# A new hand-written order for the opening of a fused attention and bilinear-FFN kernel

## The chip, the cores and the metric

The kernel runs on one core of one Trainium2 chip, as one launch. The time is device microseconds of that core: the median of three runs, 401.54 us (401.34 to 401.81). Each time is one whole execution; beside it stands one profiled execution whose trace the readings come from.

## What is computed

Attention with a relative-position bias, then a bilinear feed-forward layer, for 8 batches of 8 heads, 576 positions and 64 values a head:

```python
scores = scale * np.matmul(q, k.transpose(0, 1, 3, 2))
scores = scores + bias.transpose(2, 0, 1)[None, :, :, :]   # bias from |i - j|, 32 buckets, per head
attn = softmax(scores)
x = np.matmul(attn, v)            # then heads side by side: x is 4608 x 512
a = x @ w_a                       # 512 x 1536
b = x @ w_b
out = (a * b) @ w_out             # 1536 x 512, float32
```

## The kernel before

Work is cut by batch and pair of heads: 32 pairs, four a batch, numbered p = 0 to 31. For a pair, the 576 positions are four tiles of 128 and a tail of 64. TensorE (PE) makes scores with keys on partitions (`score`, `qk`, `qkh`), ScalarE (ACT) takes their exp into bf16 tiles `at`, VectorE (DVE) multiplies these by the exponential of the bias (tables `W` and `Wt`), and PE multiplies by v with a column of ones beside it (`av`), which yields the sums. DVE divides by the sums into `XG`, and a transpose (on PE, or by DMA on the SP queue) puts the result into `xn`, from which the feed-forward part reads. That part works in chunks of 512 positions: `pa` and `pb` (four matmuls each), ACT copies `pa` into `ha` (L703), DVE multiplies `pb` by `ha` into `g` (L706), and PE multiplies `g` by `wo`.

The program has two stages. The **opening** (batches 0 and 1, pairs 0 to 7, and the first chunk of the feed-forward part) is written out by hand as a list of tokens in the string `opening`. The **steady part** behind it (pairs 8 to 31 and the other chunks) has four lists of its own and is entered with the first `score` matmul. The kernel is built under a manual schedule: each engine issues its instructions in the order in which the tokens stand, and waits at an instruction until its inputs and its buffer are there. So the list's order is the order of each engine's queue.

A token is a kind, numbers and at times an engine, `:A` for ACT and `:D` for DVE:

- `<name`: a load. Nearly all are issued on GpSimd's (POOL's) queue.
- `TQ`, `TK` (L337, L346): PE transposes q or k of a pair into PSUM; `CQ`, `CK` (L327 on ACT, L329 on DVE): the copy out of it. `TZ`, `CZ` (L377) the same for the tails of a batch.
- `S` (`qk_half` L474, `qk` L606), `E` (L480, L458), `M` (L489, L463): scores, their exp, and the multiplication by the bias table. For pairs 0 to 3 these work on halves: `S201` is pair 2, queries' half 0, keys' half 1.
- `KS`, `EK`: scores and exp of the tails' keys for pairs 0 to 3 together.
- `T` (`qk_tail` L507 to L514), `ET` (`ex_tail` L534, L535), `MT` (L551, L543): the same for a pair's tail.
- `AV` (L583 to L593), `N` (L643 to L650): product with v and division. `X` (L672) and `CX`: transposition of the result on PE and the copy into `xn`; for pairs 4 to 6, `N` issues it as DMA transposes on SP's queue (L658, L661).
- `FA`, `HA`, `FB`, `G`: a unit of the feed-forward part: `pa`, `ha`, `pb`, `g`. The suffix is `a` or `b` for a half chunk of 256 positions and `f` for the whole 512.
- `w1`, `w2`: one or two matmuls on zeros, which fill PE's time (`warm`).
- `P..`: writes of zeros into paddings. `V`: copies of v. `LH`, `LV`: loads for batch 2; `TH`: DMA transposes of batch 2's k and q for the steady part.

What ties the tokens to each other is PSUM. One bank, `trb`, has two halves that `tr_half` hands out by turns: to TQ, to TK from pair 4 on, TZ, X, and for pairs 4 to 7 also to a small piece of T (64 tail keys against 64 tail queries, L514). The next but one in this row must wait until the first has been copied out. Scores have two tiles (pool `ps_sc`), `pa` and `pb` two banks (`ps_ff`), `av` one bank. The pieces of T and ET that matter here are:

```python
pt = ps[:, 1, n:n + 2 * ST] if n < SM else tr_half().bitcast(FP32)[:, 0:2 * ST]
nc.tensor.matmul(out=pt, lhsT=z[:, 1, :], rhs=z[:, 0, :], start=True, stop=True)   # L514
...
nc.scalar.activation(out=at[:, m:m + 2 * ST], in_=pt, func=ACTF.Exp, scale=scale)  # L534
```

PE works on different parts of its array in different tokens. Rows and columns in use, as the profile prints them: scores 64*128, transposes of q and k 128*64 (64*64 for q of pairs 0 to 3 but the first), tails' transposes 64*128, all others 128*128.

Of the kernel before, what the change touches and what calls it, by code (L numbers as in the profile page):

```python
# [13 lines left out]
def kernel(  # L14
# [774 lines left out]
    def v_next(s):  # L789
# [7 lines left out]
    ACT = nc.scalar  # L797

    opening = """
        <q123h0 <k1 <tk <vtb <k23 <W1 <W0 <v0 <vta <tq <W2 <W3 <v1 <Wta <q123h1 <R0 <Wtb <R1 <k4 <wa0  # L800
        <wb0 <R2 <uq <q5 <q4 <R3 <k5 <wa1 <q7 <wb1 <k6 <uk <k7 <vb1a <vb1b <vt1a <q6 <wb2 <vt1b <wa2 <wo
        PC0:A PX0:D YQ0:A PC1:A PU0:D PV0:A PX1:D TQ0 YK0:D TK0 CQ00:A CQ01:D CK0:D TQ10 PF1:A CQ10:D
        S000 E000 PV1:D S001 E001 TK1 CK1:D TQ30 TZ1 CZ1:D S011 CQ30:D E011 S101 TQ20 CQ20:D E101 M101
        S100 E100 TK3 CK3:D KS EK M000 TK2 S301 E301 CK2:D w2 S200 E200 M100 M001 w1 S201 E201 V0:D
        PU1:D w2 S300 E300 M200 M201 AV00 TZ0 AV10 S010 CZ0:A N00 T0 N10 E010 X10 X00 CX00:A V1:D AV20
        CX10:A TQ11 TQ21 M301 M300 ET0 AV30 CQ11:A S110 CQ21:A N20 M010 M011 PW:A MT0 S111 TQ31 E110 X20
        CQ31:A E111 T1 ET1 N30 M110 X30 CX20:D CX30:D AV01 T2 TK4 M111 S210 ET2 E210 FA0a HA0a N01 T3
        MT1 X01 AV11 CK4:D CX01:A PF0:D LH ET3 N11 S211 E211 FB0a FA1a HA1a X11 G0a MT2 CX11:D S310 E310
        FB1a G1a S311 M210 FA2a FB2a HA2a E311 TQ5 TQ4 CQ4:A M211 FA3a AV21 CQ5:A S42 G2a S43 FB3a TZ0x
        MT3 M311 HA3a M310 TK5 E42 N21 FA4a HA4a CZ0x:D AV31 LV CK5:D X21 E43 TQ7 CQ7:A G3a N31 S41 E41  # L810
        S52 E52 FB4a FA5a HA5a CX21:D G4a M43 TK6 X31 CX31:D FB5a S40 E40 CK6:D S53 G5a FA0b HA0b TZ1x
        M41 CZ1x:D FB0b G0b S51 E53 FA1b HA1b TK7 FB1b FA2b E51 M52 HA2b CK7:D S50 G1b V2:D FB2b FA3b
        E50 V3:D G2b HA3b T4 M40 FB3b G3b S70 M42 ET4 MT4 FA4b FB4b T5 HA4b M53 E70 G4b TQ6 ET5 M51
        CQ6:A AV40 N40 FA5b S71 E71 S73 MT5 M50 FB5b HA5b AV41 S72 E73 G5b N41 M71 FA6f M73 T6 E72 M72
        ET6 MT6 AV50 FB6f HA6f N50 S62 S61 E62 G6f M62 FA7f HA7f AV51 N51 TH S60 E61 M61 FB7f G7f E60
        M60 S63 E63 FA8f HA8f T7 ET7 M63 M70 FB8f G8f AV60 FA9f FB9f N60 MT7 AV70 HA9f G9f FA10f HA10f
        FB10f N70 AV71 G10f FA11f HA11f FB11f N71 X71 AV61 X70 G11f N61 CX71:D CX70:D
    """

    h0 = (0, 1)  # L820
# [292 lines left out]
```

## Time and profile before

| | |
|---|---|
| median of three runs | 401.54 us |
| the profiled execution | 401.12 us |
| its span | 399.3 us |
| PE busy | 390.6 us, 98% of the span |
| ACT busy | 255.9 us, 64% |
| DVE busy | 240.9 us, 60% |
| first matmul of the feed-forward part | 27.45 us |
| first `score` matmul, where the steady part begins | 70.84 us |

The span runs from the first instruction to the last one of the profile; some 1.8 us of the execution lie around it. Busy time of PE is modelled: a matmul's row lasts longer than its step, since the next one starts before it ends, so the price of a matmul is read from start to start.

### The profile page before, as it was taken

The numbers are of one execution on the slowest core, as the hardware profiler recorded it, in microseconds if no ns is written. First come the engines' busy times: TensorE is split into PE (matmuls) and PEld (weight loads), VectorE is DVE, ScalarE is ACT, GpSimd is POOL, SyncE is SP. The second block draws the span as 40 slices with busy tenths as digits, with TensorE's granted clock in tenths as the row PEclk, the third lists the DMA queues.
The fourth block names the chain that finished last, engine by engine and source line by source line (L and its number), as shares of the span: only waits on it lengthen the run. The fifth ranks groups of instructions, "written<-read, shape, count | busy, mean of one in ns | idle before, by whom it ended". The sixth has DMA issues, their size and how long they took to land.

```text
span 399.3 us, 13162 instructions
## 1 busy us (share of the span) xinstructions
PE 390.6 (98%) x5614; PEld 231.2 (58%) x5626; DVE 240.9 (60%) x565; ACT 255.9 (64%) x386; POOL 133.4 (33%) x199
## 2 busy tenths in 40 slices
PE   6999999999999999999999999999999999999996
PEld 2477655566665666566656665666666654444443
DVE  4799997547754775477756875487547752321420
ACT  4898994568766876587748774777568733323321
POOL 5966531739751885019700880000000000000000
PEclk9999999999999999999999999999999999999999
DMA  8999999899996999729992999161420012002004
GB/s 140 185 204 198 205 158 133 82 188 132 154 152 130 107 168 120 151 57 140 128 123 69 139 122 151 56 99 26 99 80 19 17 29 108 2 26 79 2 0 105
DMA packets 136618, 42.78 MB, mean 107 GB/s; under 512 B 114184, under 2 KB 131816, under 8 KB 136560
## 3 DMA queue, kind: packets, MB, share of 16 engines
q0 software_dynamic: 81120, 19.88, 54.5%
q1 hardware_dynamic: 50096, 12.76, 23.3%
q10 hardware_dynamic: 5344, 9.31, 7.1%
q8 instruction: 44, 0.72, 0.8%
q14 instruction: 14, 0.11, 0.1%
HBM read 39.23 MB, written 9.45 MB: 122 GB/s over the span
## 4 chain that ended last, share of the span: by engine, by line
PE 95%; DMA 1%; ACT 1%; DVE 0%; issue 0%; ACTq 0%; SPq 0%
PE ffn_pair L606 25%; PE ffn L606 24%; PE av L606 8%; PE pb L696 8%; PE pa L696 8%; PE score L606 7%; PE po L733 6%; PE av L589 2%; PE qkh L474 1%; DMA xn<-in_k_dram 1%; PE qk L606 1%; PE qr L444 1%; PE av L583 1%; PE trb L337 1%; PE trk L337 1%; ACT ath L480 0%
## 5 line engine op out<-in xcount | busy, mean ns | idle before, releaser
L458 ACT ACTIVATE at<-score 128x1024 bf16<-128x1024 f32 x96 | 98.4, 1025 | 36.7 <-PE score L606 33.3
L463 DVE TENSOR_TENSOR at<-at,W 128x1024 bf16<-128x1024 bf16 x112 | 74.7, 686 | 26.4 <-ACT at L458 18.1
L606 PE MATMUL ffn_pair<-xn,wb 64*128 64x512 bf16 x288 | 81.8, 376 | 0.0
L606 PE MATMUL ffn_pair<-xn,wa 64*128 64x512 bf16 x288 | 81.8, 376 | 0.0
L606 PE MATMUL ffn<-xn,wa 64*128 64x512 bf16 x288 | 79.9, 377 | 0.0
L606 PE MATMUL ffn<-xn,wb 64*128 64x512 bf16 x288 | 79.6, 375 | 0.0
L606 PE MATMUL av<-vm,at 64*128 64x65 bf16 x1536 | 63.4, 190 | 0.0
L606 PEld LDWEIGHTS <-at 64*128 64x128 bf16 x1536 | 48.8, 94 | 21.8 <-issue 1.2
L606 PEld LDWEIGHTS <-wa 64*128 64x128 bf16 x576 | 47.0, 94 | 17.5
L606 PEld LDWEIGHTS <-wb 64*128 64x128 bf16 x576 | 47.3, 94 | 11.6 <-issue 0.7
L706 DVE TENSOR_TENSOR g<-pb,ha 128x512 bf16<-128x512 f32 (+1 forms) x42 | 25.8, 615 | 44.7 <-PE pb L696 44.2
L606 PEld LDWEIGHTS <-g 64*128 64x128 bf16 x624 | 33.4, 94 | 24.1 <-issue 0.4
L606 PE MATMUL ffn_pair<-wo,g 64*128 64x512 bf16 x336 | 44.0, 376 | 0.0
L703 ACT ACTIVATE ha<-pa 128x512 f32<-128x512 f32 (+1 forms) x42 | 22.6, 538 | 31.9 <-PE pa L696 28.0
L138 POOL DMA_DIRECT2D qn<-in_q_dram x48 | 36.0, 781 | 11.2 <-DMA wo<-in_moe_w_out_dram 7.3
L696 PE MATMUL pb<-xn,wb 128*128 128x512 bf16 (+1 forms) x165 | 37.9, 349 | 0.3
L606 PE MATMUL score<-QB,KB 64*128 64x512 bf16 x192 | 37.9, 376 | 0.0
L696 PE MATMUL pa<-xn,wa 128*128 128x512 bf16 (+1 forms) x163 | 37.5, 348 | 0.2
L147 POOL DMA_DIRECT2D kn<-in_k_dram x48 | 35.8, 759 | 3.4 <-issue 2.2
L606 PE MATMUL av<-vm,att 64*128 64x65 bf16 x384 | 36.6, 190 | 0.0
L706 DVE TENSOR_TENSOR g<-ffn_pair,ha 128x512 bf16<-128x512 f32 x36 | 24.9, 692 | 18.5 <-ACT ha L703 18.0
L606 PE MATMUL ffn<-wo,g 64*128 64x512 bf16 x288 | 35.0, 376 | 0.0
(125 smaller groups left out, 603.1 us busy)
## 6 DMA issues: line engine op xcount, KB each, us to landing
out_dram<-QKT ACTq DMA_DIRECT2D x32, 256.0 KB, 2.0
vn<-in_v_dram POOLq DMA_DIRECT2D x16, 256.0 KB, 5.4
kn<-in_k_dram POOLq DMA_DIRECT2D x48, 64.0 KB, 4.7
qn<-in_q_dram POOLq DMA_DIRECT2D x48, 64.0 KB, 4.2
wa<-in_moe_w_a_dram POOLq DMA_DIRECT2D x3, 512.0 KB, 8.4
wb<-in_moe_w_b_dram POOLq DMA_DIRECT2D x3, 512.0 KB, 8.3
wo<-in_moe_w_out_dram POOLq DMA_DIRECT2D x1, 1536.0 KB, 16.2
xn<-XG SPq DMA_TRANSPOSE x54, 3.9
```

Of the source, the lines that this page charges most:

```text
L138: nc.gpsimd.dma_start(out=by_tile(qn[b % 2])[:, h0 // 4, t, :, :], in_=q[b, h0:h1, 128 * t:128 * t + 128, :].transpose([1, 0, 2]))
L147: nc.gpsimd.dma_start(out=by_tile(kn[b % 2])[:, h0 // 4, t, :, :], in_=k[b, h0:h1, t:SM:NM, :].transpose([1, 0, 2]))
L337: nc.tensor.transpose(ps[64 * hh:64 * hh + 64, 128 * t:128 * t + 128], src[b][:, o:o + 64], ident[:, :])
L444: nc.tensor.matmul(out=rows[hh][:, ST * t:ST * t + ST], lhsT=kT[r, t, :], rhs=z[r, 0, ST * hh:ST * hh + ST], start=True, stop=True)
L458: nc.scalar.activation(out=at[:, :, :], in_=ps[:, :, :], func=ACTF.Exp, scale=scale)
L463: nc.vector.tensor_tensor(out=at[:, :, :], in0=at[:, :, :], in1=w[:, :, S - 1 + t:S - 1 + t - SM:-1], op=MULT)
L589: nc.tensor.matmul(out=pav[:, slot, hh, :], lhsT=weights(p, t, hh, jq), rhs=vm[i][:, 2 * hp + hh, t, :], start=False, stop=True, skip_grou ...
L606: i = nc.tensor.matmul(out=o, lhsT=lhs[r], rhs=rhs[r], start=first, stop=last, skip_group_check=True)
L696: nc.tensor.matmul(out=ps[:, 0:n], lhsT=w[df // 4][:, mc, 128 * (df % 4):128 * (df % 4) + 128], rhs=xn_sb[mc][:, 512 * c + lo:512 * c + lo ...
L703: nc.scalar.activation(out=ha[:, 0:n], in_=ff["pa", df, lo][:, 0:n], func=ACTF.Copy)
L706: nc.vector.tensor_tensor(out=g_sb[df][:, lo:lo + n], in0=ff["pb", df, lo][:, 0:n], in1=ff["ha", df, lo][:, 0:n], op=MULT)
L733: nc.tensor.matmul(out=po[:, :], lhsT=g_sb[df][:, 128 * tt:128 * tt + 128], rhs=wo_sb[:, df, :], start=(df == 0), stop=(df == NDF - 1))
```

## The change

The list `opening` is written anew. Its 357 tokens are the same but for the engine of thirteen copies and pads: CZ0, CX00, CX10, CQ11, CQ31, CX01 and PF1 go from ACT to DVE; CX30, CK5, CX11, CX21, CX71 and CX70 from DVE to ACT. The loads stand first in the same order. All else moves: the order of pairs in the scores, where the feed-forward units stand among them, and that feed-forward units 6, 8 and 10 now come ahead of others with lower numbers. The steady part is unchanged.

```diff
@@ -797,24 +797,26 @@
     ACT = nc.scalar
 
     opening = """
-        <q123h0 <k1 <tk <vtb <k23 <W1 <W0 <v0 <vta <tq <W2 <W3 <v1 <Wta <q123h1 <R0 <Wtb <R1 <k4 <wa0
-        <wb0 <R2 <uq <q5 <q4 <R3 <k5 <wa1 <q7 <wb1 <k6 <uk <k7 <vb1a <vb1b <vt1a <q6 <wb2 <vt1b <wa2 <wo
-        PC0:A PX0:D YQ0:A PC1:A PU0:D PV0:A PX1:D TQ0 YK0:D TK0 CQ00:A CQ01:D CK0:D TQ10 PF1:A CQ10:D
-        S000 E000 PV1:D S001 E001 TK1 CK1:D TQ30 TZ1 CZ1:D S011 CQ30:D E011 S101 TQ20 CQ20:D E101 M101
-        S100 E100 TK3 CK3:D KS EK M000 TK2 S301 E301 CK2:D w2 S200 E200 M100 M001 w1 S201 E201 V0:D
-        PU1:D w2 S300 E300 M200 M201 AV00 TZ0 AV10 S010 CZ0:A N00 T0 N10 E010 X10 X00 CX00:A V1:D AV20
-        CX10:A TQ11 TQ21 M301 M300 ET0 AV30 CQ11:A S110 CQ21:A N20 M010 M011 PW:A MT0 S111 TQ31 E110 X20
-        CQ31:A E111 T1 ET1 N30 M110 X30 CX20:D CX30:D AV01 T2 TK4 M111 S210 ET2 E210 FA0a HA0a N01 T3
-        MT1 X01 AV11 CK4:D CX01:A PF0:D LH ET3 N11 S211 E211 FB0a FA1a HA1a X11 G0a MT2 CX11:D S310 E310
-        FB1a G1a S311 M210 FA2a FB2a HA2a E311 TQ5 TQ4 CQ4:A M211 FA3a AV21 CQ5:A S42 G2a S43 FB3a TZ0x
-        MT3 M311 HA3a M310 TK5 E42 N21 FA4a HA4a CZ0x:D AV31 LV CK5:D X21 E43 TQ7 CQ7:A G3a N31 S41 E41
-        S52 E52 FB4a FA5a HA5a CX21:D G4a M43 TK6 X31 CX31:D FB5a S40 E40 CK6:D S53 G5a FA0b HA0b TZ1x
-        M41 CZ1x:D FB0b G0b S51 E53 FA1b HA1b TK7 FB1b FA2b E51 M52 HA2b CK7:D S50 G1b V2:D FB2b FA3b
-        E50 V3:D G2b HA3b T4 M40 FB3b G3b S70 M42 ET4 MT4 FA4b FB4b T5 HA4b M53 E70 G4b TQ6 ET5 M51
-        CQ6:A AV40 N40 FA5b S71 E71 S73 MT5 M50 FB5b HA5b AV41 S72 E73 G5b N41 M71 FA6f M73 T6 E72 M72
-        ET6 MT6 AV50 FB6f HA6f N50 S62 S61 E62 G6f M62 FA7f HA7f AV51 N51 TH S60 E61 M61 FB7f G7f E60
-        M60 S63 E63 FA8f HA8f T7 ET7 M63 M70 FB8f G8f AV60 FA9f FB9f N60 MT7 AV70 HA9f G9f FA10f HA10f
-        FB10f N70 AV71 G10f FA11f HA11f FB11f N71 X71 AV61 X70 G11f N61 CX71:D CX70:D
+        <q123h0 <k1 <tk <vtb <k23 <W1 <W0 <v0 <vta <tq <W2 <W3 <v1 <Wta <q123h1 <R0 <Wtb <R1 <k4
+        <wa0 <wb0 <R2 <uq <q5 <q4 <R3 <k5 <wa1 <q7 <wb1 <k6 <uk <k7 <vb1a <vb1b <vt1a <q6 <wb2
+        <vt1b <wa2 <wo
+        PC0:A PX0:D YQ0:A PC1:A PU0:D PV0:A PX1:D TQ0 YK0:D TK0 CQ00:A CQ01:D TK1 CK0:D TQ10 S000
+        TQ20 CQ10:D CK1:D S001 E000 TK2 CQ20:D S100 E001 TZ1 E100 S101 PV1:D CK2:D CZ1:D E101 M000
+        TK3 M100 S200 E200 TQ30 M101 S010 E010 V0:D CQ30:D w2 S201 PU1:D KS E201 CK3:D w1 EK S300
+        TZ0 E300 M200 M001 w2 S301 M201 AV10 CZ0:D T0 V1:D AV00 E301 TQ21 S011 ET0 M300 N10 M301
+        N00 CQ21:A TQ11 S210 X10 E011 CQ11:D E210 AV20 X00 S211 M010 AV30 M011 N20 CX10:D PW:A E211
+        CX00:D MT0 T1 ET1 X20 CX20:D N30 TQ31 LH S111 AV01 CQ31:D MT1 E111 X30 M111 CX30:A S110
+        S310 E110 N01 TK4 E310 FA2a FA1a M110 T2 X01 S311 HA2a HA1a ET2 FB1a CX01:D AV11 E311 CK4:D
+        M211 G1a T3 N11 FB2a TQ5 G2a ET3 TQ4 CQ4:A MT2 FA0a M210 FA3a S41 CQ5:A M310 S42 HA0a M311
+        E41 E42 TZ0x TK5 MT3 AV21 FB3a N21 HA3a CK5:A S43 CZ0x:D S40 E40 E43 FB0a AV31 LV X11 X21
+        G3a FA4a CX11:A G0a HA4a N31 S51 S53 M40 X31 CX31:D FB4a CX21:A G4a TQ7 M43 TZ1x FA2b
+        CZ1x:D FA6f E51 CQ7:A HA2b FB6f E53 HA6f T4 G6f FB2b G2b V2:D T5 ET4 ET5 TK7 FA0b CK7:D
+        FA1b MT4 TQ6 TK6 HA0b M42 HA1b S72 V3:D S50 CQ6:A M41 E50 FB1b E72 G1b CK6:D FB0b G0b M53
+        AV40 FA3b S52 S60 FA5a N40 PF0:D PF1:D MT5 HA3b FB5a E52 AV41 HA5a FB3b T6 M51 G5a M52 G3b
+        FA8f E60 FB8f N41 ET6 M50 S71 S62 HA8f G8f E71 E62 AV50 M72 FA4b MT6 HA4b FB4b S61 E61 S63
+        N50 E63 M60 FA5b G4b AV51 FA10f M62 T7 N51 TH HA5b M63 HA10f FB10f M61 FB5b S73 ET7 G10f
+        S70 G5b FA7f AV60 M71 E73 MT7 M73 E70 FA11f M70 HA7f N60 FB7f HA11f AV71 G7f FA9f N71 HA9f
+        FB11f AV70 FB9f X71 G11f N70 G9f AV61 CX71:A X70 N61 CX70:A
     """
 
     h0 = (0, 1)
```

## The prediction

> **What bounds the kernel now.** I read the chain that ended last first, then the busy time by stage, then TensorE (PE) in order of time in the opening, and last what PE waited for there.
>
> ```profile
> PE 95%; DMA 1%; ACT 1%; DVE 0%; issue 0%; ACTq 0%; SPq 0%
> ```
> ```profile
> 0.00:8.00 8.00, 5.16 (x32) 1.87 (x32) 3.66 (x18) 3.95 (x8) 3.78 (x9) 1.00 0.94 154
> 8.00:17.00 9.00, 8.31 (x84) 4.09 (x79) 6.45 (x15) 6.91 (x8) 8.48 (x13) 1.00 1.06 143
> 17.00:27.00 10.00, 9.18 (x180) 6.90 (x179) 9.02 (x25) 9.80 (x17) 7.22 (x10) 1.00 1.26 216
> 27.00:49.00 22.00, 21.95 (x283) 15.20 (x279) 19.91 (x59) 19.99 (x33) 14.77 (x20) 1.00 1.35 202
> 49.00:71.00 22.00, 21.79 (x262) 13.23 (x264) 18.80 (x49) 15.01 (x22) 5.19 (x8) 1.00 1.36 141
> ```
> In the second view the columns are length, then busy us of PE, PE's weight load, DVE, ACT and POOL. PE carries 95% of the chain. From 27 us to the opening's end (first `score` matmul, 70.84 us) it is full, and the steady part behind it runs without a gap: a microsecond that PE gains or loses in the opening reaches the end whole. ACT is the fullest engine from 17 to 27 us (9.80 of 10); DVE and ACT are both near 20 of 22 from 27 to 49, so cover is thin there.
>
> **Price of a change of rows and columns.**
> ```profile
> 39.23 0.61 PE L696 MATMUL pb<-xn,wb 128*128 128x256 bf16 x4
> 39.67 0.60 PE L696 MATMUL pa<-xn,wa 128*128 128x256 bf16 x4
> 40.20 0.41 PE L337 MATMUL trb<-cn_sb,kn 128*64 128x128 bf16 x8
> ...
> 40.73 0.60 PE L696 MATMUL pb<-xn,wb 128*128 128x256 bf16 x4
> 41.26 0.60 PE L606 MATMUL qk<-QKT 64*128 64x512 bf16 x4
> ```
> Columns: start, length, rows*columns, shape. Four matmuls of one form, followed by the same form, take 0.44 us from start to start (39.23 to 39.67); followed by another form, 0.53 (39.67 to 40.20, 40.73 to 41.26). A change costs 0.53 - 0.44 = 0.09; over all such pairs of the opening at full rate I find 94 to 101 ns, and use 95.
>
> **Term 1, fewer changes: -1.4.** In the built order the opening has 76 changes before and 61 after. Ahead of the first FFN matmul (27.45 us in the trace) there are 32 in both; the 15 that go lie behind it, where PE is full: 15 x 95 ns = 1.43 us. The matmuls are the same 826; the loads and SP's transposes keep their order.
>
> **Term 2, a new wait at TK7: +1.5.** For pairs 4 to 7, `T` (qk_tail) puts a small piece into one half of the transposes' bank `trb`, and `ET` (ex_tail) reads it first (L534) and then does the large exp (L535). Before, T4, ET4, T5, TQ6, ET5 stand with other work between:
> ```profile
> 46.94 0.22 PE L514 MATMUL trb<-ZB 128*128 128x128 bf16 x1
> ...
> 49.17 0.22 PE L514 MATMUL trb<-ZB 128*128 128x128 bf16 x1
> 49.32 0.41 PE L337 MATMUL trb<-cn_sb,qn 128*64 128x128 bf16 x8
> ```
> ```profile
> 47.19 0.28 ACT L534 ACTIVATE att<-trb 128x128 bf16<-128x128 f32 x1
> 47.37 1.02 ACT L535 ACTIVATE att<-qkt 128x1024 bf16<-128x1024 f32 x1
> ```
> TQ6 (49.32) needs T4's half, which ACT had read since 47.47: no wait. In the new order T5, ET4, ET5, TK7 follow at once. In the built program ET4's small exp waits for T5's last matmul (PE raises no count between), and TK7's first transpose waits for a count that ACT raises only behind ET5's small exp. From the start of T5's last matmul: 0.25 to the small exp (46.94 to 47.19), 0.18 to the large one, 0.91 until the next can start (two exps last 1.93 at 39.29, one 1.02), 0.28 for ET5's small exp, 0.06 back to PE: 1.68 us. Without the wait TK7 would start 0.056 + 0.095 later: 1.53 us are new, and behind TK7 on PE stands all the rest. ACT cannot start earlier, whatever it has done before, so only a part hidden by a later PE could shorten it: I see none.
>
> **Term 3, waits at TQ7 and FB6f: +1.1 (0 to 1.3).** TQ7 takes the half of `trb` that X21 filled; CX21 now empties it on ACT, and in the built program waits for CX31 on DVE (both read the bank). From CK5's start the chain by rows is CK5 0.67 with its hand-over, CZ0x 0.55, G3a and G0a 2 x 0.34, N31 1.0, M40 0.61, CX31 0.39, CX21 0.55, hand-over 0.1: 4.5. Beside it PE has FB0a 0.53, AV31 0.90, X11 and X21 0.3, FA4a 0.53, S51 and S53 0.53, X31 0.2, FB4a 0.53: 3.5, and some 0.2 ahead of FB0a. So 0.8 is left. Likewise FB6f wants the bank that HA2b empties, and HA2b stands on ACT behind CQ7, which waits for CZ1x on DVE: about 0.3. At the low end DVE is ahead and both vanish; the high end is 4.5 - 3.5 plus that 0.3.
>
> **Term 4, the last AVs: +0.3 (0 to 1.0).** N70's writes to XG1 wait until the DMA transposes of pair 5 have read it. Their landing was at 67.19 us, 6.7 us after issue, with N71 at 68.85. AV51, from which they follow, stands 13.1 us ahead of the opening's end (57.76 to 70.84) and by the rows some 12.7 in the new order, so the landing moves back by the microsecond PE loses, while N71 and N70 stand earlier: about 0.8 of DVE wait, of which PE's AV70 and AV61 see 0.3.
>
> **Term 5, the first 27 us: -0.2 (-0.9 to +0.8).**
> ```profile
> PE qkt L507 <- ACT ath L480: 0.6, 1, 0.6
> PE warm L248 <- issue: 0.3, 1, 0.3
> PE trb L346 <- ACT xn L327: 0.3, 1, 0.3
> PE qkh L474 <- DVE QKT L329: 0.2, 1, 0.2
> ```
> These are all of PE's long waits from 8 us on. ACT sets the pace; ahead of the first `ha` copy it had 14 full exps, 3 tail exps and 8 copies (14 x 0.92 + 3 x 0.82 + 8 x 0.27 = 17.5 us) and gets 16, 2 and 3 (17.2): -0.3. Against that, the new order has three waits of PE on `trb`'s two halves in place of two (X20 behind CX10 and CX00, behind N20 on DVE; TQ31 behind CX20). TQ11 also needs the second half of q, landed at 19.51 us, so a faster start is cut off there. I take -0.2; the low end removes the 0.6 and 0.3 at L507 and L346, the high end adds one more wait of 0.6 and 0.2.
>
> **Sum.** -1.4 + 1.5 + 1.1 + 0.3 - 0.2 = **+1.3 us**. The profiled execution took 401.12 us (span 399.3, 1.8 around it), 0.4 under the median of 401.54; so 402.4 beside that one and **402.8** as a median. 0.2% is 0.8 us, about what a measurement of this kernel can tell from no change.
>
> **Rivals.**
> *DVE keeps up.* Terms 3 and 4 vanish because PE, having waited early, comes later to TQ7: -1.4 + 1.5 - 0.2 = -0.1, 401.4. For it: DVE has 2 us of idle in 27 to 49. Against: the copies stand behind N31 and M40.
> *Faster: the first 27 us shrink.* Old ACT stood idle 2.1 us between 8.96 and 28.6 (19.6 less 17.5); if the new order fills that, term 5 is -2.4, and with DVE keeping up the sum is -1.4 + 1.5 - 2.4 = -2.3: 399.2. It decides from a gain of 0.7 beyond the forecast's -0.2 with terms 3 and 4 gone. Against: the 19.51 us landing.
> *The rate.* PEclk reads full throughout, yet five 512-wide warm matmuls took 2.31 us at 1.19 (0.43 each) and two took 0.61 at 17.58: PE ran at half rate until about 17.0, 4.9 us after 12.14, where it had become nearly full. If TK7's 1.5 us of idle brought half rate back for as long, that costs 4.9 / 2 = 2.4: 405.2. Against: 0.56 us of idle at 24.86 changed nothing. The Trainium skill, TensorE: Matmul & The Clock Gate, Part 1, has the rate fall only after about 3.4 us idle, so not here; no run here shows it yet. By its free-running window, half rate could also end one window later, half of 3.4 us more: an estimate of 404.5.
> *Later transposes.* If pair 5's landing slips by a further 1 us, PE waits for it whole: 403.8.
> *A dearer change.* A 256-wide matmul lasts 0.16 us beyond its 0.109 us step (0.60 - 3 x 0.109 = 0.27). If a change of form cost all of that, term 1 would be 15 x 0.16 = 2.4, the sum +0.3 and the time 401.8. Against: the 94 to 101 ns of every pair that I found. The Trainium skill, TensorEngine Tiling (Array Packing), Key Properties, says that changing the mode drains the engine; the trace shows 0.095 us for it and not the whole 0.16.
> *The change does not do what it says:* excluded, 76 and 61 are counted in the built orders.
>
> **Numbers.** Forecast 0.57 (own range 402.3 to 403.7), DVE keeps up 0.17, dearer change 0.05, shorter start 0.08, rate 0.06, transposes 0.07. Faster 0.08; same 0.17 + 0.05 = 0.22; slower 0.57 + 0.06 + 0.07 = 0.70. The range runs from DVE keeping up, 401.4, to 404.3, past the late transposes; it leaves out the start's case and the rate's.
>
> **What would show it.** Right: PE idle for about 1.5 us before TK7's transposes (L337), released by ACT's L534, one of about 0.8 before TQ7, and the first `score` matmul near 72.1 us against 70.84. Wrong: no PE gap over 0.5 us behind 27 us, or `score` before 70.8; matmuls of 0.43 us per 512 behind 17 us would mean the rate.

## The result and the profile after

The changed kernel took **403.95 us** (median of 7 runs, 402.33 to 404.42); the kernel before took 401.46 us in 7 runs beside it (400.47 to 403.03). The ratio is 1.0057 (95% interval 1.0036 to 1.0079), so the new order is slower by some 2.5 us. The forecast was 402.8 us with a range of 401.4 to 404.3. A later repeat (the last experiment) gave 403.03 against 400.86, 2.2 us more. The profiled execution of the changed kernel took 404.36 us (span 402.6), that of the kernel before 401.12 (span 399.3).

The chain that ended last, by engine, changed kernel:

```profile
PE 85%; DVE 5%; DMA 3%; ACT 2%; POOL 1%; issue 1%; ACTq 1%; DVEq 0%
```

The chain had 95% on PE before. It now leaves PE for DVE, the loads and ACT, so the opening has places where PE is not what ends last. Busy time by stage (length, then busy us of PE, PE's weight load, DVE, ACT and POOL):

```profile
17.00:27.00 10.00, 7.80 (x154) 5.73 (x153) 9.49 (x27) 7.70 (x10) 8.19 (x12) 1.00 1.25 215
27.00:49.00 22.00, 19.29 (x262) 13.82 (x259) 16.31 (x49) 18.82 (x33) 14.02 (x19) 1.00 1.36 200
49.00:73.00 24.00, 23.92 (x290) 15.30 (x289) 21.83 (x57) 17.14 (x28) 5.92 (x9) 1.00 1.19 137
```

From 17 to 27 us the roles have changed sides: ACT had 9.80 of 10 before and has 7.70, DVE had 9.02 and has 9.49. From 27 to 49 us PE had 21.95 of 22 and has 19.29; behind 49 us it is full again. What PE waited for between 8 and 74 us (total, times, longest):

```profile
PE trb L337 <- ACT att L534: 1.5, 1, 1.5
PE trb L337 <- ACT xn L327: 1.0, 1, 1.0
PE qkt L507 <- DVE ZB L329: 0.7, 1, 0.7
PE trb L672 <- DVE xn L329: 0.5, 1, 0.5
PE trb L346 <- DVE xn L329: 0.5, 1, 0.5
...
PE pb L696 <- ACT ha L703: 0.3, 1, 0.3
```

The first two and the last are those that the prediction named: TK7, TQ7 and FB6f. The three between lie ahead of 27 us: T0, X20 and TQ31. On PE's timeline (start, length, then idle time ahead and its releaser in brackets):

```profile
41.45 0.41 PE L337 MATMUL trb<-cn_sb,qn 128*64 128x128 bf16 x8 [0.95 <-ACT xn L327]
...
43.80 1.02 PE L696 MATMUL pb<-xn,wb 128*128 128x512 bf16 x4 [0.31 <-ACT ha L703]
...
47.75 0.41 PE L337 MATMUL trb<-cn_sb,kn 128*64 128x128 bf16 x8 [1.45 <-ACT att L534]
```

and on ACT's, the instructions that release the first and the third of these:

```profile
40.83 0.57 ACT L327 ACTIVATE xn<-trb 128x256 bf16<-128x256 bf16 x2 [1.10 <-DVE xn L329]
...
47.41 0.29 ACT L534 ACTIVATE att<-trb 128x128 bf16<-128x128 f32 x1
```

TK7 starts 0.34 us after ET5's small exp (L534 at 47.41), which is the order of events that the prediction laid out. Where a wait is followed from start to start, less the step and the 0.095 of a change, the three cost 1.02 (TQ7), 0.47 (FB6f) and 1.52 us (TK7).

A profiled execution of the opening has three parts: up to the first feed-forward matmul (`pa`), from there to the first `score` matmul, and the rest.

| | `bl_sb` landed | first W load issued | q's second half landed | `pa` | `score` | `pa` to `score` | `score` to end |
|---|---|---|---|---|---|---|---|
| before | 2.98 | 8.52 | 19.51 | 27.45 | 70.84 | 43.39 | 328.5 |
| changed | 3.67 | 9.55 | 20.52 | 28.33 | 73.54 | 45.21 | 329.0 |

`bl_sb` is a small part of the bias table that DVE subtracts before anything else of the table can be made. Of the 3.2 us between the spans, 1.82 lie between `pa` and `score` (terms 1 to 4 made it 1.5), 0.88 ahead of `pa` (term 5 made it -0.2), and 0.5 behind `score`, where the program is the same (other profiles scatter by more there, see below). So two questions stood: whether the three waits are what they look like, and why the first part came out late. The theory for the first: they come from the order in which copies and writes of one bank stand. For the second, two rivals: the execution's small load landed late by chance (3.67 against 2.98) and the new order passes such a delay on; or single waits that the new order has there (T0's 0.7, X20's 0.5) set it.

### The profile page after: what moved, and what is told of

Same layout as the page of the kernel before. It is cut to its first block, busy times and chain, and to the rows that moved or that the text cites. A ratio compares the mean times of both kernels' runs of the same rounds, so it can differ in the third digit from the quotient of the medians.

```text
span 402.6 us, 13175 instructions
## 1 busy us (share of the span) xinstructions
PE 390.1 (97%) x5626; PEld 230.6 (57%) x5626; DVE 240.8 (60%) x565; ACT 256.1 (64%) x386; POOL 133.3 (33%) x199
## 4 chain that ended last, share of the span: by engine, by line
PE 85%; DVE 5%; DMA 3%; ACT 2%; POOL 1%; issue 1%; ACTq 1%; DVEq 0%
PE ffn_pair L606 24%; PE ffn L606 24%; PE av L606 8%; PE pb L696 7%; PE score L606 7%; PE pa L696 6%; PE po L733 6%; DVE at L463 2%; DMA qn<-in_q_dram 1%; DMA bias_tab<-wo 1%; PE av L589 1%; DVE g L706 1%; PE qr L444 1%; DMA bl_sb<-in_bias_table_dram 1%; POOL W L263 1%
## 5 line engine op out<-in xcount | busy, mean ns | idle before, releaser
L463 DVE TENSOR_TENSOR at<-at,W 128x1024 bf16<-128x1024 bf16 x112 | 74.9, 686 | 27.2 <-ACT at L458 19.0
L706 DVE TENSOR_TENSOR g<-pb,ha 128x512 bf16<-128x512 f32 (+1 forms) x42 | 25.6, 614 | 45.4 <-PE pb L696 42.7
L706 DVE TENSOR_TENSOR g<-ffn_pair,ha 128x512 bf16<-128x512 f32 x36 | 24.9, 691 | 18.5 <-ACT ha L703 18.0
```

The source lines that it names most:

```text
L463: nc.vector.tensor_tensor(out=at[:, :, :], in0=at[:, :, :], in1=w[:, :, S - 1 + t:S - 1 + t - SM:-1], op=MULT)
L706: nc.vector.tensor_tensor(out=g_sb[df][:, lo:lo + n], in0=ff["pb", df, lo][:, 0:n], in1=ff["ha", df, lo][:, 0:n], op=MULT)
```

## Experiments

Edits are to the changed kernel's list unless the kernel before is named, and only the pieces of the list that differ are shown; the rest of the program is as it was. Each ratio is against runs of the kernel before on the same chip.

**TK7 moved ahead of ET5.**

```diff
-T4 G6f FB2b G2b V2:D T5 ET4 ET5 TK7
+T4 ET4 G6f FB2b G2b V2:D T5 TK7 ET5
```

> The new order with two tokens moved: ET4 directly behind T4, and TK7 ahead of ET5 (T4 ET4 G6f FB2b G2b V2 T5 TK7 ET5). Theory (the wait at TK7 is added time on the full engine): TensorE's idle of 1.5 us before TK7's transposes goes, and the time falls by 1.2 to 1.5 us against the new order, to about the time of before (+0.8 to +1.2 us against it, since the first part stays late). Rival (some other engine is late next and takes the gain back): the idle goes, but the first score matmul comes less than 0.5 us earlier than 73.5 us, and the time stays 2 us or more above before.

Measured: 402.3 us (12 runs) against 401.2; ratio 1.0032 (1.0017 to 1.0046). From `pa` to `score` it took 43.72 us, 1.49 less than the changed kernel. By the medians it is 1.1 us over before, in place of 2.2 to 2.5; the intervals of the ratios overlap a little, so the trace's 1.49 is the surer figure. PE's and ACT's timelines of this kernel:

```profile
45.16 0.22 PE L514 MATMUL trb<-ZB 128*128 128x128 bf16 x1
45.30 0.41 PE L337 MATMUL trb<-cn_sb,kn 128*64 128x128 bf16 x8
```
```profile
45.76 0.28 ACT L534 ACTIVATE att<-trb 128x128 bf16<-128x128 f32 x1
```

TK7 follows T5's last matmul by 0.14 us, ahead of ET5's small exp (45.76): the wait is gone from the trace, and its 1.5 us with it. Term 2 is the cost of this one position.

**M40 behind CX31**, to empty `trb` sooner for TQ7.

```diff
-G0a HA4a N31 S51 S53 M40 X31 CX31:D FB4a CX21:A G4a TQ7
+G0a HA4a N31 S51 S53 X31 CX31:D M40 FB4a CX21:A G4a TQ7
```

> The new order with M40 moved behind the copy CX31, for which TQ7 waits by way of CX21. Theory (TQ7 waits for a chain of VectorE): the chain is shorter by one multiplication, 0.61 us, so the wait at TQ7 falls from 1.0 to about 0.4 us and the time by up to 0.6 us. Rival (the same delay comes back at the next hand-over between VectorE and ScalarE, at FB6f, because both read the transposes' bank by turns): the wait at FB6f grows by what TQ7's loses, and the time falls by less than 0.2 us.

Measured: 404.29 us (6 runs); ratio 1.0076 (1.0054 to 1.0099). TQ7's idle time went only from 0.95 to 0.80, FB6f's rose from 0.31 to 0.39, and `pa` to `score` took 45.15 us, 0.06 less than in the changed kernel. Rows of DVE, ACT and PE of this kernel:

```profile
38.82 0.39 DVE L329 COPY xn<-trb 128x256 bf16<-128x256 bf16 x2 [0.56 <-PE trb L672]
```
```profile
39.31 0.60 ACT L327 ACTIVATE xn<-trb 128x256 bf16<-128x256 bf16 x2 [0.93 <-DVE xn L329]
```
```profile
39.95 0.41 PE L337 MATMUL trb<-cn_sb,qn 128*64 128x128 bf16 x8 [0.80 <-DVE at L463]
```

DVE now stands idle for 0.56 until X31 is there; ACT waits 0.93 for DVE; PE starts 0.64 after ACT. (The profile names DVE's L463 as releaser, which ended at 39.93; CX21's end on ACT, 39.91, is as near, and it is what empties the half.) The theory that M40's 0.69 on DVE makes this wait is wrong: without M40, CX31 starts 0.44 us behind X31's start (38.38), with it 0.62 (39.72 to 40.34 in the changed kernel), so M40 costs 0.18. The chain X31, CX31, CX21, TQ7 lasts 1.6 us by itself (38.38 to 39.95), and PE has only FB4a's 0.44 beside it. This profiled execution also had one idle stretch of 1.8 us on PE far behind in the steady part, put down to no engine; the time is not explained by it alone, and I draw nothing from the 0.3 us by which it stands above the changed kernel.

**CQ11 on ACT**, so that X20 need not wait for it on the fuller DVE.

```diff
-TQ11 S210 X10 E011 CQ11:D
+TQ11 S210 X10 E011 CQ11:A
```

> The new order with one copy of the first 27 us, CQ11, given back to ScalarE. VectorE is busy 9.5 of 10 us from 17 to 27 us there, ScalarE 7.7. Theory (the seven copies and pads that went from ScalarE to VectorE made VectorE the bound of the first part): the waits at X20 and TQ31 (0.7 and 0.5 us) shrink and the first feed-forward matmul comes 0.3 to 0.7 us earlier. Rival (the first part is late because its loads landed a microsecond later in this execution): less than 0.2 us.

Measured: 403.13 us (11 runs); ratio 1.0045 (1.0032 to 1.0058). X20's wait is gone, TQ31's 0.5 stayed. `pa` stood at 27.48, with `bl_sb` landed in time (3.04) but q's second half as late as 20.24, for which TQ11 waited 0.3. That is earlier than the 28.33 of the first profile, but not earlier than the 27.40 and 26.98 of the two runs above, which have the changed list as far as `pa` and the table in time. So the theory that these copies made DVE the bound is not shown by this run, and the gain in time is not to be told from nothing by these intervals.

**Both of these.**

> The new order with both: ET4 behind T4, TK7 ahead of ET5, and CQ11 on ScalarE. If the two gains add up: 1.6 to 2.1 us under the new order, so 0.3 to 0.8 us above before or, where the loads land as early as in the trace of before, 0.2 to 0.7 us below it. Rival (the last transposes of pair 5, for whose landing N70 waits, hold what is won): the wait of the AVs at the opening's end grows by 0.5 us or more, and the time is that of the run with TK7 apart alone.

Measured: 401.88 us (12 runs); ratio 1.0010 (0.9996 to 1.0024). The waits at TQ7 (0.96), FB6f (0.31), TQ31 (0.47) and T0 (0.57) are left. From `pa` to `score` it took 43.74 us, 0.35 more than before: the fifteen fewer changes nearly pay for TQ7 and FB6f. The two gains add up about as expected (1.5 to 1.8 us less over before than the changed kernel, 1.6 to 2.1 expected), and no new wait came at the opening's end.

**The bias table later on purpose**, in the new order and in the old. Three more writes of the table's background, which repeat one that the kernel has already done, stand ahead of DVE's subtraction of `bl_sb`; they add work and change no result.

```diff
+    for _ in range(3):
+        nc.vector.memset(tab_sb.bitcast(FP32)[0:H, :], TWO_ONES)
```

New order:

> The new order with the bias table made late: three more writes of the table's background (0.48 us each on VectorE) stand ahead of the subtraction that starts it, so that the first load of W goes out some 0.9 us later and every load behind it on POOL's queue too. In the profile of the new order that load went out 1.03 us later than before (9.55 against 8.52 us), because a small load for the table landed at 3.67 instead of 2.98 us, and the first feed-forward matmul came at 28.33 us against 27.45. Theory (the new order passes a late table on to the end, since VectorE stands first for M200 and TQ11 for the second half of q): the first feed-forward matmul comes at 28 us or later and the time is 0.5 to 1.0 us above the new order's 403.95. Rival (the lateness of the first part came from the order itself): within 0.3 us of it.

Old order:

> The order of before with the same three writes, so the same late table. Theory (the old order reaches the uses of W2 and of the second half of q later, and absorbs it): the first feed-forward matmul within 0.3 us of 27.45 and the time within 0.4 us of before. Rival (a late table costs any order as much): 0.8 to 1.0 us above before.

Measured: new order 404.38 us (6 runs) against 401.14, ratio 1.0074 (1.0048 to 1.0100); old order 400.74 (12 runs) against the same 401.14, 0.9993 (0.9976 to 1.0011). The first W load went out at 9.29 and 9.41. `pa` stood at 28.03 in the new order, at 26.72 in the old. Busy time from 17 to 27 us, old order with the late table:

```profile
17.00:27.00 10.00, 9.11 (x182) 7.11 (x181) 9.30 (x26) 9.90 (x18) 7.72 (x12) 1.00 1.21 207
```

With the table 0.9 us later than in its first profile the old order still fills ACT (9.90) and loses nothing: `pa` is even 0.7 earlier than in that profile. The new order passes the delay on: 28.03, against 26.98 and 27.40 with the table in time. This is seen at `pa`, in one profile of each; in the times of the new order it is not clear, since its ratio of 1.0074 and the changed kernel's 1.0057 and 1.0052 have intervals that overlap.

**Is it one wait?** CZ0 ahead, for T0:

```diff
-TZ0 E300 M200 M001 w2 S301 M201 AV10 CZ0:D T0
+TZ0 E300 CZ0:D M200 M001 w2 S301 M201 AV10 T0
```

> The new order with the copy CZ0, for which T0's scores wait, ahead of the three multiplications M200, M001 and M201 on VectorE. Theory A (T0's wait of 0.9 us is what makes the first part late): the first feed-forward matmul comes up to 0.9 us earlier. Theory B (VectorE as a whole, or the landing of the second half of q, sets the first part): the idle time only moves, to TQ11 or to the AVs behind, and the time changes by less than 0.3 us or gets longer by up to 0.8 us.

q's second half ahead, for TQ11:

```diff
-<W2 <W3 <v1 <Wta <q123h1
+<W2 <W3 <q123h1 <v1 <Wta
```

> The new order with the load of the second half of q ahead of v's second half and the first tail table on POOL's queue, two issues of 0.7 us earlier. Theory A (TQ11's wait for it, 0.3 us at 20.57, is on the path): the wait goes and the first feed-forward matmul comes 0.3 us earlier. Theory B (VectorE sets the first part): no more than 0.1 us.

Measured: 404.45 us (6 runs), ratio 1.0075 (1.0049 to 1.0101), and 403.93 (7 runs), 1.0065 (1.0042 to 1.0088): no gain from either. In both the chosen wait went, and another came. PE's waits, first and second kernel:

```profile
PE av L583 <- DVE XG L645: 0.9, 1, 0.9
```
```profile
PE av L583 <- DVE XG L645: 0.8, 1, 0.8
```

AV20 now waits for DVE's division (L645). In both of these executions `bl_sb` also landed late (3.51 and 3.77), and `pa` stood at 28.75 and 28.48. So they speak for the late table alone: there DVE as a whole, with the loads that it waits for (0.95 us for W and 0.71 for v in the second kernel), sets the pace, and which token of PE shows it is a matter of detail.

**The price of a change, measured by itself.** In the kernel before, a matmul of 64 columns on zeros stands ahead of each group of four `pa` or `pb` in the opening, 36 in all; its result is overwritten at once. First with 128 rows, which makes no change, then with 64 rows, which adds 37.

```diff
+        if c == 0:
+            nc.tensor.matmul(out=ps[:, 0:64], lhsT=zero_sb[0:128, 0:128], rhs=zero_sb[0:128, 0:64],
+                             start=True, stop=True)
```

> The order of before with one more matmul, of zeros, at the head of each of the 36 feed-forward units of the opening: 128 rows, 128 columns, 64 wide, into the unit's own bank, which the unit then overwrites. No change of rows and columns is added (75 ahead of the first score matmul, as before). By the step of such a matmul, some 30 ns, it adds 36 x 0.03 = 1.1 us on a full TensorE: 0.8 to 1.3 us above before. If the opening were held by another engine, nothing.

> The same 36 matmuls with 64 rows in use in place of 128: the same number of instructions and the same width, but 112 changes of rows and columns in place of 75. Theory (a change costs 95 ns of a full TensorE): 37 x 0.095 = 3.5 us above the run with 128 rows. Rival (a change costs the whole 0.16 us that a matmul lasts beyond its step): 5.9 us. Rival (most changes are hidden behind waits): under 1.5 us.

Measured: 402.76 us (7 runs), ratio 1.0042 (1.0024 to 1.0060), `pa` to `score` 44.44 (1.05 more than before, 29 ns a matmul); and 406.67 (4 runs), 1.0145 (1.0120 to 1.0170), `pa` to `score` 48.35. The second has 3.91 us more in both measures. That is 106 ns for each of the 37 changes by the medians, and 103 ns from `pa` to `score`, where 38 of the changes lie (its first zero matmul, the mark `pa`, has the form of what stands ahead of it): **103 to 106 ns each**. The first kernel's time is 1.85 us above before, over the 0.8 to 1.3 expected; its part behind `score` was longer (329.9 us against 328.5), with which the difference of the two kernels has nothing to do (329.9 in both). PE's timeline with 128 rows, then with 64:

```profile
43.60 0.60 PE L699 MATMUL pb<-xn,wb 128*128 128x256 bf16 x4
44.04 0.19 PE L696 MATMUL pa<-zero_sb 128*128 128x64 bf16 x1
44.07 0.60 PE L699 MATMUL pa<-xn,wa 128*128 128x256 bf16 x4
```
```profile
45.22 0.61 PE L699 MATMUL pb<-xn,wb 128*128 128x256 bf16 x4
45.76 0.20 PE L696 MATMUL pa<-zero_sb 64*128 64x64 bf16 x1
45.89 0.61 PE L699 MATMUL pa<-xn,wa 128*128 128x256 bf16 x4
```

From `pb` to the next `pa` it takes 0.47 us with one form and 0.67 with two changes: 0.10 each.

**TQ7 as well.** To the edits of the fourth experiment, CX21 comes ahead, with more of PE's work beside it:

```diff
-X11 X21 G3a FA4a CX11:A G0a HA4a N31 S51 S53 M40 X31 CX31:D FB4a CX21:A G4a TQ7 M43 TZ1x FA2b
-CZ1x:D FA6f E51 CQ7:A HA2b FB6f
+X11 X21 G3a FA4a CX11:A CX21:A G0a HA4a N31 S51 S53 X31 TQ7 CX31:D CQ7:A M40 FB4a G4a FA2b
+HA2b TZ1x CZ1x:D M43 FA6f E51 FB6f
```

> The order with TK7 apart and CQ11 on ScalarE, and in addition CX21 ahead of X31, TQ7 directly behind X31 and ahead of CX31, M40 behind both, and TZ1x behind FA2b. No copy of the transposes' bank then stands in the list between X21's copy and TQ7. Theory (a write into that bank waits for every copy that stands ahead of it in the list): the wait of 0.96 us at TQ7 and that of 0.3 us at FB6f go, and the time falls by 0.8 to 1.2 us against the order with TK7 and CQ11 alone, to 400.7 to 401.1, some 0.2 to 0.5 us under before. Rival (the delay moves to the next write into the bank, TZ1x or T4, because VectorE and ScalarE copy no faster): a new wait of 0.5 us or more stands there, and the time falls by less than 0.4 us.

Measured: 401.26 us (12 runs) against 400.86; ratio 1.0006 (0.9991 to 1.0022). What PE waited for is short again: behind 27 us only this is left of the long ones,

```profile
PE trb L377 <- ACT QKT L327: 0.3, 1, 0.3
```

and `pa` to `score` took 42.92 us, 0.82 less than with the fourth experiment's edits and 0.47 less than before. The time did not follow as expected: it is 0.4 us above before, in place of 0.2 to 0.5 below, and 0.3 less over before than in the fourth experiment, in place of 0.8 to 1.2. The intervals are too wide to tell either from nothing. The profiled execution (400.04 us, `pa` at 26.54) was the fastest of the twelve. This order has 62 changes, one more than the changed kernel; without the long waits it is no faster than the one it replaced, within what is measured.

**The changed kernel once more**, unchanged, to see its start in another execution.

> The new order once more, unchanged, timed beside the run above and profiled again. Theory (the first part is late only where the small load for the bias table lands late): with that landing near 3.0 us in this profile the first feed-forward matmul comes near 27.2 us and the first score matmul near 72.4; with a landing over 3.5 us near 28.3 and 73.5. The median again 2 to 3 us above before, since the wait at TK7, TQ7 and FB6f stand in every execution. Rival: 28.3 us with an early landing too.

Measured: 403.03 us (12 runs, 402.19 to 405.23) against 400.86; ratio 1.0052 (1.0036 to 1.0068). In its profiled execution (403.05 us) `bl_sb` landed at 2.98, `pa` stood at 27.20 and `score` at 72.44:

```profile
17.00:27.00 10.00, 8.85 (x175) 6.50 (x174) 8.98 (x27) 8.81 (x12) 6.95 (x10) 1.00 1.25 205
```

With the table in time PE has 8.85 of 10 in this stage, against 7.80 in the first profile. From `pa` to `score` it is the same as there (45.24 and 45.21). The waits at X20 and TQ31 (0.5 each) stand in both.

## Why the prediction was right, and where its sizes were off

**Term 1, the changes: right.** Forecast 95 ns each and 1.4 us; measured 103 to 106 ns by itself, so 15 of them are 1.4 to 1.6 us. The dearer change (0.16) is excluded, since 37 of those would have been 5.9 us and not 3.91.

**Term 2, TK7: right.** Forecast 1.53, measured 1.52, and 1.49 came back when TK7 was moved. The mechanism was the one laid out.

**Term 3, TQ7 and FB6f: right in place, too small.** Forecast 0.8 and 0.3, measured 1.02 and 0.47, so 1.5 in place of 1.1 and above the high end of 1.3. The path from CK5 to TQ7 was right, but it lasted 4.9 us (36.52 to 41.45) in place of 4.5, since nearly every link took up to 0.1 longer; PE's 3.5 beside it held, and began 0.46 behind CK5 in place of 0.2. To take out M40 does not help: CX31 then has to wait for X31 itself. The rival that DVE keeps up falls: the hand-overs from PE to DVE to ACT to PE set the wait, whether DVE has idle time or not.

**Term 4, the last AVs: wrong mechanism, small.** Forecast 0.3; no AV waited. Pair 5's last transposes were issued at 63.86 and landed at 66.08, in 2.2 us and not in the 6.7 of before. What was late was another place: FA7f's first `pa` came 0.15 late behind DVE's `g` (L706).

Together: -1.43 + 1.52 + 1.49 + 0.15 = 1.73, against 1.82 measured between `pa` and `score` (1.85 in the repeat).

**Term 5, the first 27 us: not settled.** Forecast -0.2. The first profile gave +0.9, with the table late, and the repeat -0.25, with the table in time. One profile is little to go by: four executions of the old order, of which three have edits that do not touch that part or only delay the table, put `pa` at 27.45, 26.72, 26.26 and 26.67 (mean 26.78), and three of the new list as far as `pa`, with the table in time, at 27.40, 26.98 and 27.20 (mean 27.19). The difference of +0.4 is no larger than the scatter within one order, so its sign is not shown. That 27.45 was a late start does not show in the time either: that execution took 401.12 us, among medians of 400.86 to 401.54.

What is shown is the late table. With it the new order came to `pa` at 28.0 to 28.8 in four profiles (two of them of the lists with CZ0 or q's load moved), the old order at 26.72 in one. There the term's premise, that ACT sets the pace, failed: ACT is down to 7.70 of 10 and DVE at 9.49, and DVE's queue begins with the table. With the table in time no engine of the new order is full from 17 to 27 us (PE 8.85, DVE 8.98, ACT 8.81 in the repeat), so the five copies that went to DVE ahead of `pa` did not make it the bound there. Their work shows at X20, whose wait of 0.5 went when CQ11 went back to ACT; TQ31's 0.5 stayed. The prediction had named these two waits but kept them for its high end; they stand in every profile that has the changed list as far as `pa`.

So of the 0.9 to 1.2 us by which the time went beyond +1.3, the part from `pa` to `score` explains 0.3 (term 3 took 0.4 more, term 4 0.15 less). The rest lies ahead of `pa` and behind `score`, and how much of it is the order's own stays open.

**The rate: did not come.** Behind TK7's 1.5 us of idle a feed-forward unit goes on at its full step; no matmul of 0.43 us per 512 shows behind it:

```profile
48.10 1.05 PE L696 MATMUL pa<-xn,wa 128*128 128x256 bf16 x8
49.08 0.41 PE L337 MATMUL trb<-cn_sb,qn 128*64 128x128 bf16 x8
```

Eight matmuls 256 wide and one change take 0.98 us, as 8 x 0.109 + 0.1 would. The sentence of the Trainium skill (TensorE: Matmul & The Clock Gate, Part 1) by which the rate falls only after some 3.4 us of idle agrees with that, but another execution differs, and the measurement decides. In the profile of the kernel before with the 36 matmuls of 128 rows, eight transposes of k take 0.41 us at 6.95 and 0.64 at 8.46, as at half rate, though PE's longest idle stretch between 5.0 and 8.5 us was 1.55:

```profile
6.95 0.41 PE L337 MATMUL trk<-cn_sb,kn 128*64 128x128 bf16 x8 [1.55 <-DVE kn L329]
...
8.46 0.64 PE L337 MATMUL trk<-cn_sb,kn 128*64 128x128 bf16 x8
```

The granted clock of that profile reads 0.50 from 12 to 15 us. So the rival was not excluded by the length of TK7's wait; that the rate held behind it is what this trace shows. The prediction's estimate of 404.5 with half rate one window longer does not describe what happened, since PE came to full rate at 14.2 us in the changed kernel, earlier than the 17.25 of before, and was later at `pa` all the same.

**Direction and range.** It came out slower, as forecast; 403.95 lies inside the range, above the forecast's own 402.3 to 403.7, and the repeat's 403.03 within it. That the range reached beyond 403.7 was owed to pair 5's late transposes, which did not come; so far it held by luck. What stays open besides: why `bl_sb` lands up to 0.8 us late in some executions (only profiled ones show it, so how often it happens among the timed runs is not known), and what makes the part behind `score`, which is the same program in all, longer or shorter: 329.0 and 328.8 us in the two profiles of the changed kernel, 328.5 in that of before, and 328.4 to 329.9 in ten of the variants (the eleventh, M40 behind CX31, has 330.7 with its idle stretch of 1.8). The 0.3 to 0.5 us of the changed kernel are within this scatter.

## What to carry to other kernels

When an order of instructions is made to save a small price many times, look first at each place where a bank or buffer changes hands: follow who writes it next and which copies stand ahead of that write in the list, since one such place (1.52 us) cost as much as fifteen changes of 95 to 106 ns saved. When copies move from one engine to another, ask which input the new engine's queue begins with and whether that can be late; the old bound's spare time does not answer this. And one profile of before is one sample of its start: compare several before a term of some tenths of a microsecond is read from it.

## What the runs showed of the hardware that was not expected

- The first small load's landing varies between executions of the same program (`bl_sb`, 2.94 to 3.77 us in these profiles) and moves a whole queue of later loads with it: POOL's first load of W was issued at 8.15 to 8.54 us where it landed early and at 9.15 to 9.55 where it landed late or the subtraction was held up; in the changed kernel's first profile q's second half landed 1.0 us later than before. Changed kernel, POOL and DVE:

```profile
9.55 0.72 POOL L263 DMA_DIRECT2D W<-bias_tab  x1 [4.74 <-DMA bias_tab<-wo]
```
```profile
3.77 0.15 DVE L242 TENSOR_TENSOR bt_sb<-bt_sb,bl_sb 32x8 f32<-32x8 f32 x1 [1.26 <-DMA bl_sb<-in_bias_table_dram]
```

- The moment at which PE reaches its full rate varies by nearly 5 us: 12.5 and 12.75 us in the earliest profiles, 17.25 before, and 14.2 and 17.43 in two executions of the changed kernel. In the old order it seems to show at `pa`: 26.26 with full rate from 15.42, 26.72 from 15.88, 26.67 from 16.57, 27.45 from 17.25. So it does in the new order with CQ11 on ACT and the table in time: 26.54 from 12.50, 27.07 from 14.51, 27.48 from 16.89. The late table weighs more: 28.03 with full rate from 12.75. In the profiles of before and of the changed kernel the row of the clock reads full throughout, so there the rate is seen only from start to start. Changed kernel, PE, the last group at half rate and the first at full rate:

```profile
12.98 0.61 PE L474 MATMUL qkh<-QKT 64*128 64x256 bf16 x4
...
14.20 0.39 PE L474 MATMUL qkh<-QKT 64*128 64x256 bf16 x4
```

- A DMA transpose's time from issue to landing (6.7 us before, 2.2 in the changed kernel, for the same tile) is not a property of its size. What makes it was not tried.
